# Attention sums and values of two head groups together on 64 by 32 TensorE tiles, in a kernel of attention and a two-layer MLP

## The chip, the cores and the metric

The kernel runs on one core of a Trainium2 chip. The metric is the device time of one execution in microseconds (us). Five runs of the kernel before gave 445.26 to 445.73 us, with a median of 445.7. Profiles come from one execution; in a profile "span" is the time from the first to the last instruction.

A core has five engines that run side by side, each working through its own list of instructions in order: TensorE (PE; its weight loads are shown as PEld), VectorE (DVE), ScalarE (ACT), GpSimd (POOL) and SyncE (SP). TensorE writes to PSUM, which here is cut into eight banks of 128 partitions by 512 fp32.

## What is computed

```
q_n = q / sqrt(mean(q*q) + 1e-6) * g_q        # the same for k; head_dim 64
attn = softmax(q_n k_n^T / 8)                 # 8 batches, 12 heads, 448 x 448
x    = (attn v) as [8*448 tokens, 768]
h    = x @ w_in                               # 768 x 2048
g    = max(h, 0) + alpha * min(h, 0)
out  = g @ w_out                              # 2048 x 768, fp32
```

All inputs are fp32. The kernel multiplies in fp16.

## The kernel before

**Groups.** Four heads make a group: two in each of two halves `g` of the head list (heads i and i+6 lie in different halves), and in each half two heads, `par` 0 and 1. There are G = 3 groups per batch and NG = 24 in all, counted y = 3*b + i. A key block j has 64 keys; J = 7 blocks make 448.

**One group's steps.** `load_qk` (L93, issued by SP) brings q and k. `square` (L128, POOL), `reduce` (L138, DVE), `root` (L146, ScalarE) and `scale` (L155, POOL) normalise them. They are then transposed, so that the head dimension lies on partitions: for y < TD = 8 on TensorE with 14 transposes and two evacuations (`turn`, L175), for later groups by two DMA transposes that SP issues (`turn_dma`, L165); `turn` is then only a multiply by the gain, in place, on DVE.

`score(y, j)` (L212) does four matmuls of 64 by 64, one for each head: keys go to PSUM partitions, the 448 queries are columns. The four use the four 64 by 64 tiles of the array at the same time. `soft` (L226) is one exp on ScalarE over 128 x 896, from PSUM to the fp16 tile `expT`. Score tiles have two PSUM buffers of two banks.

`den` (L250) sums over the keys, with weights of ones (64 columns, so each sum stands in 64 partitions); `attv` (L263) is the same with v as weights. Both are done by `over_keys` (L234): 28 matmuls of 64 by 64 by 448 columns, accumulated over j. Their result lies in `acc`, a two-bank buffer of which there is one. `log` and `invert` (L254, L259; ScalarE) make 1/sum as exp(-ln). DVE multiplies values by that into `xT`, the fp16 input of the MLP.

**MLP.** `up(b, ft)` (L307): six matmuls of 128 x 128 x 448 into one bank, ScalarE makes alpha*h, DVE takes the maximum and writes `gT`. `down(b0, t, oh)` (L322): 16 matmuls of 128 x 128 x 384 for 128 tokens and half `oh` of the output columns; DVE copies to `osb`, SP stores. Banks come from a pool of two (`psf`, tag "mm"), or, where `spare` is set, from `acc`.

**The order.** It is written out by a planner (L360 to L469), not found by a scheduler. The attention is cut into bursts. A burst has two score tiles (three where it also does sums or values from group 3 on), and possibly one group's sums (`dens`) or values (`avs`). Between bursts stand the `ups` and `downs` that the planner deals out by estimated costs (`gaps`, L434 to L462). There are 66 bursts. The burst in which batch 0's last group is summed is the "lead" (burst 11): there the MLP starts. Preparation of a later group is put into bursts by number: `prep` runs ahead of a burst, `post` behind it, `roots` and `jobs` inside. Lines 518 to 604 then emit all of it.

**Weights.** POOL issues the loads that convert fp32 to fp16: v of a batch (`load_v`, two requests), w_in in four parts by columns (`load_w_in`), w_out in four parts by rows (`load_w_out`). All of them go through one queue, whose transfers follow one another.

At the start TensorE multiplies idle data (`spin`, L348) between the first bursts.

Of the kernel before, what the change touches and what calls it, by code (L numbers as in the profile page):

```python
# [21 lines left out]
def kernel(  # L22
# [26 lines left out]
    TD = min(8, NG)  # L49
# [22 lines left out]
    ones = cst.tile([128, 64], FP16, name="ones", tag="ones")  # L72
# [3 lines left out]
    idle = cst.tile([128, S], FP16, name="idle", tag="idle")  # L76
    nc.vector.memset(idle, 0.0)
# [9 lines left out]
    gT = cst.tile([128, NF, W], FP16, name="gT", tag="gT")  # L87

# [26 lines left out]
    def load_w_in(c):  # L115
        nc.gpsimd.dma_start(
            out=w_in_sb[:, :, ts(c, FB)],
            in_=moe_w_in[:, ts(c, FB)].rearrange("(k p) f -> p k f", p=128),
        )

    def load_w_out(c):
        nc.gpsimd.dma_start(
            out=w_out_sb[:, ts(c, NF // 4), :],
            in_=moe_w_out[ts(c, DF // 4), :].rearrange("(t p) m -> p t m", p=128),
        )
# [86 lines left out]
    def score(y, j):  # L212
        qT, kT = qkT[y, "q"], qkT[y, "k"]
        sc = pss.tile([128, 2, 512], FP32, name="sc", tag="sc")
        for par in range(2):
            for g in range(2):
                nc.tensor.matmul(  # L217
                    out=sc[ds(64 * g, 64), par, :S].rearrange("p (j c) -> p j c", j=J),
                    lhsT=kT[ds(64 * par, 64), j, g, :],
                    rhs=qT[ds(64 * par, 64), :, g, :],  # L220
                    start=True,
                    stop=True,
                )
        scs[y, j] = sc

    def soft(y, j):  # L226
        if j == 0:
            expT[y] = att.tile([128, J, 2, S], FP16, name="expT", tag="expT")
        nc.scalar.activation(  # L229
            out=expT[y][:, j], in_=scs[y, j][:, :, :S], func=AF.Exp,  # L230
            scale=QK_SCALE, bias=expb[:, 0:1],
        )

    def over_keys(name, y, weights, spare=False):  # L234
        pool, tag = (pss, "sc") if spare else (psa, "acc")
        acc = pool.tile([128, 2, 512], FP32, name=name, tag=tag)
        e = expT[y]
        for j in range(J):
            for g in range(2):
                for par in range(2):  # L240
                    nc.tensor.matmul(  # L241
                        out=acc[ds(64 * par, 64), g, :S],
                        lhsT=weights(g, par, j),
                        rhs=e[ds(64 * g, 64), j, par, :],
                        start=(j == 0),
                        stop=(j == J - 1),
                    )
        return acc

    def den(y):  # L250
        dn = over_keys("dn", y, lambda g, par, j: ones[ds(64 * g, 64), :])
        rden[y] = dn

    def log(y):  # L254
        r = att.tile([128, 2, S], FP32, name="rden", tag="rden")
        nc.scalar.activation(out=r, in_=rden[y][:, :, :S], func=AF.Ln)  # L256
        rden[y] = r

    def invert(y):  # L259
        r = rden[y]  # L260
        nc.scalar.activation(out=r, in_=r, func=AF.Exp, scale=-1.0)  # L261

    def attv(y, spare=False, jobs=()):  # L263
        b, i = divmod(y, G)
        vv = vt[b]
        av = over_keys(
            "av", y, lambda g, par, j: vv[ds(64 * g, 64), 2 * i + par, j, :], spare
        )
        for f in jobs:
            f(y)  # L270
        if i == 0:
            xT[b] = att.tile([128, 2, G, S], FP16, name="xT", tag="xT")
        nc.vector.tensor_mul(  # L273
            out=xT[b][:, :, i, :], in0=av[:, :, :S], in1=rden[y]
        )
# [44 lines left out]
    osb = {}  # L320

    def down(b0, t, oh, jobs=(), spare=False):  # L322

        op = bank("op", spare)
        for ft in range(NF):
            nc.tensor.matmul(  # L326
                out=op[:, :OH],
                lhsT=gT[:, ft, ts(t, 128)],
                rhs=w_out_sb[:, ft, ds(oh * OH, OH)],
                start=(ft == 0),  # L330
                stop=(ft == NF - 1),
            )
        for f, a in jobs:
            f(*a)
        if oh == 0:
            osb[b0, t] = ffn.tile([128, DM], FP32, name="osb", tag="osb", bufs=3)
        o = osb[b0, t]
        nc.vector.tensor_copy(out=o[:, ds(oh * OH, OH)], in_=op[:, :OH])  # L338
        last = (b0, t) == (B - 2, J - 1)
        if oh == 1 or last:  # L340
            cols_out = ds(oh * OH, OH) if last else slice(None)
            for half in range(2):
                bb, j = divmod(2 * t + half, J)
                (nc.scalar if last and half else nc.sync).dma_start(
                    out=out4[b0 + bb, j, :, cols_out], in_=o[ds(64 * half, 64), cols_out]
                )
# [13 lines left out]
    bursts, dens, avs, first_in, last_in = [], {}, {}, {}, {}  # L360
    m = 0
    while m < NG * J or len(avs) < NG:
        n = len(bursts)
        if len(dens) > len(avs):
            avs[n] = len(avs)
        elif len(dens) < NG and last_in.get(len(dens), n) < n:
            dens[n] = len(dens)
            if dens[n] == G - 1:
                avs[n] = G - 1
        three = n in dens and dens[n] >= G or n in avs and avs[n] >= G  # L370
        count = min(3 if three else 2, NG * J - m)
        bursts.append([divmod(m + c, J) for c in range(count)])
        for y, j in bursts[n]:
            first_in.setdefault(y, n)
            if j == J - 1:
                last_in[y] = n
        m += count
    NB = len(bursts)
    den_at = {y: n for n, y in dens.items()}
    av_at = {y: n for n, y in avs.items()}  # L380
# [5 lines left out]
    def after(n, f, *a):  # L386
# [3 lines left out]
        y: max(n for n in range(first_in[y]) if n not in dens) for y in range(1, NG)  # L390
    }
    turn_at[2] = av_at[0]
    turns = {n: y for y, n in turn_at.items()}
    jobs = {}
    for y in range(G, NG):

        early = y < G + 2
        n = turn_at[y - 1] + (y == G) if early else max(d for d in dens if d <= turn_at[y] - 2)
        at(n - (8 if early else 5), load_qk, y)
        for nm in "qk":  # L400
            (after if early else at)(n - 2, square, y, nm)
            if early:
                after(n, reduce, y, nm)
            else:
                jobs.setdefault(n, []).append((reduce, (y, nm)))
        roots[n + 1 + (y == G + 1)] = y
# [7 lines left out]
    for b in range(B):  # L414
# [6 lines left out]
        tail = len(new) if b == B - 1 else 3 if b == 0 else 2 if odd else 1  # L421
# [3 lines left out]
    def cost(n):  # L425
        return (
            0.31 + 0.19 * len(bursts[n])
            + (1.35 if n in dens or n in avs else 0.0) + (0.9 if turns.get(n, TD) < TD else 0.0)
        )
# [6 lines left out]
    for b in range(B - 1):  # L436
# [3 lines left out]
        per = (mlp + sum(cost(n) for n in range(lo, hi))) / (hi - lo)  # L440
        clock = 0.0
        for n in range(lo, hi):
            clock += cost(n)
            free = True
            while ups or old or new:
# [14 lines left out]
                short = n in turns and len(gaps[n]) < 2  # L460
                if n < hi - 1 and not short and clock + ahead > per * (n - lo + 1):
                    break  # L462
# [42 lines left out]
    for nm in "qk":  # L505
        after(0, scale, 1, nm)
    after(0, load_w_in, 0)
    after(0, square, 2, "k")
    for nm in "qk":
        after(2, reduce, 2, nm)  # L510
    after(2, load_w_in, 1)
    after(5, load_w_in, 2)
    after(6, load_w_in, 3)
    for c in range(4):
        at(first - 2 + c, load_w_out, c)
    roots[4] = 2

    for n in range(NB):
# [5 lines left out]
        if lead:  # L524
            den(dens[n])
            attv(avs[n], True, (log, invert))
        for t in tiles[:2]:
# [4 lines left out]
            elif n == den_at[G - 1] - 1 and t == tiles[0]:  # L532
                begin(0)
# [4 lines left out]
        for t in tiles[:1] if wait else tiles[:2]:  # L538
# [3 lines left out]
        if n in avs and not lead:  # L542
            attv(avs[n])
        for t in tiles[2:]:
            score(*t)
            soft(*t)
        late = []
# [18 lines left out]
        for k, (f, a) in enumerate(gaps[n][:-1]):  # L566
            free = 2.3 if n in dens else 1.2 if n in avs else 0.1
            if clock >= free and not turns.get(n, TD) < TD and (
                not spare_at or k - spare_at[-1] > 2
            ):  # L570
                spare_at.append(k)
            clock += DOWN if f is down else UP
        ups_first = gaps[n] and gaps[n][0][0] is up
        if ups_first:
            for f, a in jobs.pop(n, ()):
                f(*a)
        turned = n in turns and turns[n] >= TD and ups_first
        if turned:
            turn(turns[n])
        for k, (f, a) in enumerate(gaps[n]):  # L580
# [3 lines left out]
            else:  # L584
                f(*a, spare)
                done += 1
                if late and done == late[0][0]:
# [3 lines left out]
            if n in turns and not turned and k == (  # L591
                0 if turns[n] >= TD or plain else max(min(1, len(gaps[n]) - 2), 0)
            ):
                turn(turns[n])
        if not gaps[n] and n in turns:
            turn(turns[n])
        for _, g, c in late:
# [37 lines left out]
```

The softmax here doesn't subtract the row's maximum and nothing guards it: scores larger than these inputs give would overflow.

## Time and profile before

| | |
|---|---|
| profiled execution, its own time | 445.36 us |
| its span | 443.6 us |
| median of five runs | 445.7 us |
| scores L217: matmuls, mean of one exp behind them | 672, 1007 ns |
| sums L241 (`dn`), values L241 (`av`): matmuls | 672, 672 |
| log, inverse: count, mean | 24 each, 928 and 953 ns |
| `turn` on TensorE: transposes | 112 |
| DVE: values times 1/sum, mean | 1091 ns |
| w_out: issue to landing, median | 20.7 us |

The page gives for each engine its busy time, then 40 equal slices of the span with the busy share of each in tenths. The longest chain of work that ends last has PE with 85% of the span, ScalarE with 8% and DVE with 4%; its largest lines are down (L326, 34%), up (L290, 29%), scores (8%), values (6%) and sums (6%). Matmuls are pipelined, and the profile models their ends: a matmul shown as 349 ns long can have a successor 47 ns later. So the time between starts is what counts on PE. Two groups of idle time look large and are not on that chain: POOL's 169.9 us ahead of `scale`, and DVE's 97.4 us waiting for a down.

### The profile page before, as it was taken

The page shows a single profiled execution, that of the slowest core. Times are in us where ns is not written, and L with a number is a line of the kernel's source. Part 1 is how long each engine was busy: PE and PEld are TensorE (multiplying, and loading weights), DVE is VectorE, ACT ScalarE, POOL GpSimd, SP SyncE. Part 2 cuts the span into 40 slices and gives each one's busy share as a digit, 9 for nine tenths or more (in the row PEclk, how much of TensorE's full clock was granted, in tenths as well). Part 3 has the DMA queues.
Part 4 walks back from the last instruction along what each step waited for, and adds up shares of the span by engine and source line. Part 5 has one row for each costly group of instructions (what it writes and reads, how often), then busy time and mean ns, then how long its engine had stood idle before and what let it go on. Part 6 is the DMA issues. An engine that isn't in the chain of part 4 may idle for free.

```text
span 443.6 us, 9091 instructions
## 1 busy us (share of the span) xinstructions
PE 424.9 (96%) x3837; PEld 228.9 (52%) x3837; DVE 206.8 (47%) x297; ACT 290.2 (65%) x401; POOL 170.8 (39%) x125
## 2 busy tenths in 40 slices
PE   7889998899999999999999999999999999999996
PEld 3344444555445555545555555545555545555563
DVE  3656654445554454454453554445553353234421
ACT  4998888667967676766875776767875767222300
POOL 4779946551554352362554351461533000000000
PEclk9899999999999999999999999999999999999999
DMA  8999999442973591771982583651732401111122
GB/s 196 230 237 245 233 252 199 120 91 72 190 159 69 129 178 46 161 124 38 196 183 62 141 163 62 161 126 36 140 78 51 63 2 38 37 35 37 35 72 71
DMA packets 60009, 52.77 MB, mean 119 GB/s; under 512 B 32688, under 2 KB 56512, under 8 KB 59968
## 3 DMA queue, kind: packets, MB, share of 16 engines
q1 hardware_dynamic: 47424, 39.27, 38.2%
q0 software_dynamic: 11808, 11.81, 16.7%
q10 hardware_dynamic: 736, 1.11, 1.0%
q8 instruction: 30, 0.49, 0.5%
q14 instruction: 11, 0.09, 0.1%
HBM read 45.62 MB, written 11.01 MB: 128 GB/s over the span
## 4 chain that ended last, share of the span: by engine, by line
PE 85%; ACT 8%; DVE 4%; DMA 1%; issue 0%; ACTq 0%
PE op L326 32%; PE hT L290 19%; PE hTa L290 10%; PE sc L217 8%; PE av L241 6%; PE dn L241 6%; ACT expT L229 4%; PE opa L326 2%; ACT ah L317 2%; DMA nat<-in_k_dram 1%; PE tps L193 1%; DVE gT L318 1%; PE spin L353 1%; ACT rden L256 1%; DVE kT L204 1%; DVE qT L202 1%
## 5 line engine op out<-in xcount | busy, mean ns | idle before, releaser
L229 ACT ACTIVATE expT<-sc,expb 128x896 f16<-128x896 f32 x168 | 158.5, 1007 | 18.4 <-PE sc L217 17.9
L326 PE MATMUL op<-w_out_sb,gT 128*128 128x384 f16 x848 | 145.6, 326 | 0.0
L158 POOL TENSOR_TENSOR qs<-nat,rr 128x896 f16<-128x896 f32 x44 | 78.1, 1795 | 169.9 <-issue 129.9
L326 PEld LDWEIGHTS <-gT 128*128 128x128 f16 x896 | 84.6, 98 | 63.5 <-issue 10.1
L290 PE MATMUL hT<-xT,w_in_sb 128*128 128x448 f16 x528 | 112.1, 353 | 2.4 <-DVE gT L318 2.4
L290 PEld LDWEIGHTS <-w_in_sb 128*128 128x128 f16 x768 | 73.4, 98 | 73.1 <-issue 9.1
L317 ACT ACTIVATE ah<-hT,cols 128x448 f16<-128x448 f32 x88 | 55.7, 634 | 62.9 <-PE hT L290 62.9
L318 DVE TENSOR_TENSOR gT<-hT,ah 128x448 f16<-128x448 f32 x88 | 54.8, 624 | 58.4 <-ACT ah L317 58.3
L338 DVE COPY osb<-op 128x384 f32<-128x384 f32 x53 | 29.5, 557 | 97.4 <-PE op L326 97.4
L135 POOL TENSOR_TENSOR sq<-nat 128x896 f32<-128x896 f32 x44 | 73.0, 1677 | 2.0 <-DMA nat<-in_k_dram 1.2
L217 PE MATMUL sc<-qT,kT 64*64 64x448 f16 x672 | 53.7, 362 | 7.0 <-DVE kT L204 3.3
L141 DVE TENSOR_REDUCE ss<-sq 128x14 f32<-128x896 f32 x48 | 49.9, 1076 | 6.9 <-ACT sq L133 6.3
L290 PE MATMUL hTa<-xT,w_in_sb 128*128 128x448 f16 x228 | 49.3, 352 | 0.0
L317 ACT ACTIVATE ah<-hTa,cols 128x448 f16<-128x448 f32 x38 | 24.1, 633 | 37.6 <-PE hTa L290 37.6
L318 DVE TENSOR_TENSOR gT<-hTa,ah 128x448 f16<-128x448 f32 x38 | 23.7, 624 | 33.8 <-ACT ah L317 33.8
L241 PE MATMUL av<-expT,vt 64*64 64x448 f16 x672 | 35.9, 349 | 1.8 <-ACT rden L256 1.8
L217 PEld LDWEIGHTS <-kT 64*64 64x64 f16 x672 | 18.6, 105 | 36.8 <-issue 25.1
L273 DVE TENSOR_TENSOR xT<-av,rden 128x896 f16<-128x896 f32 x24 | 26.2, 1091 | 21.6 <-PE av L241 19.8
L241 PE MATMUL dn<-expT,ones 64*64 64x448 f16 x672 | 36.0, 349 | 0.2 <-DVE gT L318 0.2
L241 PEld LDWEIGHTS <-vt 64*64 64x64 f16 x672 | 20.6, 107 | 13.3 <-issue 2.6
L241 PEld LDWEIGHTS <-ones 64*64 64x64 f16 x672 | 20.9, 107 | 11.1 <-issue 0.6
L261 ACT ACTIVATE rden<-rden 128x896 f32<-128x896 f32 x24 | 22.9, 953 | 0.7
(40 smaller groups left out, 136.1 us busy)
## 6 DMA issues: line engine op xcount, KB each, us to landing
out_dram<-osb SPq DMA_DIRECT2D x54, 192.0 KB, 2.7
nat<-in_q_dram SPq DMA_DIRECT2D x46, 224.0 KB, 4.7
nat<-in_k_dram SPq DMA_DIRECT2D x46, 224.0 KB, 5.4
vt<-in_v_dram POOLq DMA_DIRECT2D x16, 336.0 KB, 7.7
w_in_sb<-in_moe_w_in_dram POOLq DMA_DIRECT2D x4, 768.0 KB, 13.9
w_out_sb<-in_moe_w_out_dram POOLq DMA_DIRECT2D x4, 768.0 KB, 20.7
nat<-in_q_dram ACTq DMA_DIRECT2D x2, 224.0 KB, 4.8
nat<-in_k_dram ACTq DMA_DIRECT2D x2, 224.0 KB, 6.2
```

Source lines behind the costliest of these rows:

```text
L135: nc.gpsimd.tensor_mul(out=sqf, in0=src, in1=src)
L141: nc.vector.tensor_reduce(out=ss_t[y][:, "qk".index(nm)].rearrange("p h j -> p (h j)").unsqueeze(2), in_=sqs[y, nm], axis=AXIS_X, op=ALU.add,)
L158: eng.tensor_mul(out=t.rearrange("p j h d -> p h j d"), in0=nat[y, nm], in1=rr_t[y][:, "qk".index(nm)].unsqueeze(3).broadcast_to((128, 2, ...
L217: nc.tensor.matmul(out=sc[ds(64 * g, 64), par, :S].rearrange("p (j c) -> p j c", j=J), lhsT=kT[ds(64 * par, 64), j, g, :], rhs=qT[ds(64 * ...
L229: nc.scalar.activation(out=expT[y][:, j], in_=scs[y, j][:, :, :S], func=AF.Exp, scale=QK_SCALE, bias=expb[:, 0:1],)
L241: nc.tensor.matmul(out=acc[ds(64 * par, 64), g, :S], lhsT=weights(g, par, j), rhs=e[ds(64 * g, 64), j, par, :], start=(j == 0), stop=(j == ...
L273: nc.vector.tensor_mul(out=xT[b][:, :, i, :], in0=av[:, :, :S], in1=rden[y])
L290: nc.tensor.matmul(out=hT[:, :S], lhsT=w_in_sb[:, g * G + i, ts(ft, 128)], rhs=xT[b][:, g, i, :], start=(i == 0 and g == 0), stop=(i == G ...
L317: nc.scalar.activation(out=ah, in_=hT[:, :S], func=AF.Copy, scale=alpha_sb[:, ft : ft + 1])
L318: nc.vector.tensor_max(out=gT[:, ft, ds((b & 1) * S, S)], in0=hT[:, :S], in1=ah)
L326: nc.tensor.matmul(out=op[:, :OH], lhsT=gT[:, ft, ts(t, 128)], rhs=w_out_sb[:, ft, ds(oh * OH, OH)], start=(ft == 0), stop=(ft == NF - 1),)
L338: nc.vector.tensor_copy(out=o[:, ds(oh * OH, OH)], in_=op[:, :OH])
```

## The change

1. `over_keys` takes one or two groups. With two, the eight heads are spread over eight tiles of 64 rows by 32 columns (four column strips, two halves g), so each head has 32 partitions of the result. `den` of a pair is then one set of seven key blocks with eight matmuls each. Values of a pair take two sets: even columns of v (`half` 0) into `acc`, odd columns (`half` 1) into the two "mm" banks. A single group (the third of a batch) uses the eight tiles with the two halves of each head's 64 columns. Groups of a batch are done as a pair and a single one.
2. `score` does eight matmuls of 64 by 32 instead of four of 64 by 64.
3. In a burst with a pair's values, the third score stands between the two halves. `expT` has three buffers instead of two, `osb` two instead of three.
4. The rows of w_in are loaded in another order, since the columns of x stand in another order in `xT`: three requests per part. w_out is loaded by column halves.
5. TD is 6 instead of 8: groups 6 and 7 (the first two of the third batch) are also transposed by DMA. The bursts at which groups are loaded, squared, rooted and turned are set anew. There are 73 bursts; the lead is burst 10. The first down stays in burst 17, values of the pair (3, 4) stand in burst 18.
6. The planner's costs, and the choice of downs and ups that use the spare bank, follow the new bursts; `idle` is now a part of `gT`.

```
-    TD = min(8, NG)
+    TD = min(6, NG)
+    EB = 3
...
     def load_w_in(c):
+        src = moe_w_in[:, ts(c, FB)].rearrange("(g r) f -> g r f", g=2)
+        dst = w_in_sb[:, :, ts(c, FB)].rearrange("p (g i) f -> p g i f", g=2)
+        for g in range(2):
+            nc.gpsimd.dma_start(
+                out=dst[:, g, 0:2], in_=src[g, :256].rearrange("(p e) f -> p e f", e=2)
+            )
         nc.gpsimd.dma_start(
-            out=w_in_sb[:, :, ts(c, FB)],
-            in_=moe_w_in[:, ts(c, FB)].rearrange("(k p) f -> p k f", p=128),
+            out=dst[:, :, 2], in_=src[:, 256:].rearrange("g p f -> p g f")
         )
     def load_w_out(c):
+        oh, half = divmod(c, 2)
         nc.gpsimd.dma_start(
-            out=w_out_sb[:, ts(c, NF // 4), :],
-            in_=moe_w_out[ts(c, DF // 4), :].rearrange("(t p) m -> p t m", p=128),
+            out=w_out_sb[:, ts(half, NF // 2), ds(oh * OH, OH)],
+            in_=moe_w_out[ts(half, DF // 2), ds(oh * OH, OH)].rearrange(
+                "(t p) m -> p t m", p=128
+            ),
         )
...
+        for c in range(2):
+            for par in range(2):
+                for g in range(2):
+                    nc.tensor.matmul(
+                        out=sc[ds(64 * g + 32 * c, 32), par, :S].rearrange(
+                            "p (j c) -> p j c", j=J
+                        ),
+                        lhsT=kT[ds(64 * par, 64), j, g, ts(c, 32)],
...
+    def over_keys(accs, ys, weights):
+        if len(ys) == 2:
+            heads = [(y, par, 0) for y in ys for par in range(2)]
+        else:
+            heads = [(ys[0], par, c) for par in range(2) for c in range(2)]
         for j in range(J):
-            for g in range(2):
-                for par in range(2):
+            for h, (y, par, c) in enumerate(heads):
+                for g in range(2):
                     nc.tensor.matmul(
-                        out=acc[ds(64 * par, 64), g, :S],
-                        lhsT=weights(g, par, j),
-                        rhs=e[ds(64 * g, 64), j, par, :],
+                        out=accs[g][ds(32 * h, 32), :S],
+                        lhsT=weights(g, y, par, c, j),
+                        rhs=expT[y][ds(64 * g, 64), j, par, :],
...
+    def attv(ys, half, spare=False, jobs=()):
+        b, i = divmod(ys[0], G)
+        v2 = vt[b].rearrange("p h j (d e) -> p h j d e", e=2)
+        def weights(g, y, par, c, j):
+            h = 2 * (y - G * b) + par
+            if len(ys) == 1:
+                return vt[b][ds(64 * g, 64), h, j, ts(c, 32)]
+            return v2[ds(64 * g, 64), h, j, :, half]
+        if half:
+            av, accs = None, [psf.tile([128, 512], FP32, name="avb", tag="mm") for _ in range(2)]
...
+        x, r = xT[b][:, :, i + half, :], rden[ys]
+        if half:
+            for g in range(2):
+                nc.vector.tensor_mul(out=x[:, g], in0=accs[g][:, :S], in1=r[:, g])
+        else:
+            nc.vector.tensor_mul(out=x, in0=av[:, :, :S], in1=r)
...
     after(0, load_w_in, 0)
-    after(2, load_w_in, 1)
-    after(5, load_w_in, 2)
-    after(6, load_w_in, 3)
+    after(5, load_w_in, 1)
+    after(7, load_w_in, 2)
+    after(8, load_w_in, 3)
     for c in range(4):
-        at(first - 2 + c, load_w_out, c)
+        after(first + c // 2, load_w_out, c)
...
         if n in avs and not lead:
-            attv(avs[n])
-        for t in tiles[2:]:
+            attv(avs[n], 0)
+        for t in tiles[len(first_tiles) :]:
             score(*t)
             soft(*t)
+        if n in avs and len(avs[n]) == 2:
+            attv(avs[n], 1)
```

## Prediction

> **What bounds the kernel now.** I read the busy shares first, then the slices, then the idle time of the engines by releaser, then TensorE's order of time around one ordinary burst, and last the first 80 us by themselves.
>
> ```profile
> PE 424.9 (96%) x3837; PEld 228.9 (52%) x3837; DVE 206.8 (47%) x297; ACT 290.2 (65%) x401; POOL 170.8 (39%) x125
> PE   7889998899999999999999999999999999999996
> ...
> PEclk9899999999999999999999999999999999999999
> DMA  8999999442973591771982583651732401111122
> ```
>
> TensorE is busy and at full clock from the ninth slice on; DMA is full only in the first seven slices. So there are two stages with different limits. A busy PE need not be an efficient one, so I look at starts, in the timeline of PE:
>
> ```profile
> 201.92 1.30 PE L290 MATMUL hTa<-xT,w_in_sb 128*128 128x448 f16 x6
> 203.05 1.30 PE L290 MATMUL hT<-xT,w_in_sb 128*128 128x448 f16 x6
> 204.28 0.57 PE L217 MATMUL sc<-qT,kT 64*64 64x448 f16 x8
> 204.68 1.49 PE L241 MATMUL av<-expT,vt 64*64 64x448 f16 x28
> 206.01 0.36 PE L217 MATMUL sc<-qT,kT 64*64 64x448 f16 x4
> 206.30 2.77 PE L326 MATMUL op<-w_out_sb,gT 128*128 128x384 f16 x16
> ```
>
> From start to start: six full-array matmuls take 1.13 (189 ns each); 28 matmuls of 64 by 64 take 1.33, which is seven rounds of four tiles at once, 189 ns a round. That is one round per 448 columns, with nothing between. Only where the array changes its tiling is there more: 1.23 instead of 1.13 ahead of the scores (+0.10), 0.29 instead of 0.19 behind them (+0.10). Hence 0.2 us per burst. Here only fewer rounds help. The windows give the same:
>
> ```profile
> 21.00:41.00 20.00, 16.71 (x266) 9.45 (x264) 11.86 (x13) 19.04 (x25) 17.54 (x12) 1.00 1.16 234
> 38.10:41.10 3.00, 3.00 (x64) 1.75 (x64) 1.90 (x2) 2.28 (x4) 3.00 (x3) 1.00 1.16 269
> 46.00:83.00 37.00, 32.85 (x346) 17.57 (x349) 20.20 (x30) 29.10 (x43) 24.50 (x18) 1.00 0.99 201
> 83.00:400.00 317.00, 314.47 (x2880) 170.24 (x2873) 147.89 (x214) 217.37 (x298) 110.85 (x72) 1.00 0.49 103
> ```
>
> (columns: busy PE, PEld, DVE, ACT, POOL, then clock, DMA share, GB/s.) From 83 to 400 TensorE idles 2.5 of 317 us; from 21 to 41 ScalarE is the full one (19.0 of 20), and from 46 to 83 nobody is quite full but DMA (0.99).
>
> **The change, part by part.** All sums are against the profiled execution: span 443.6, its own time 445.36, so 1.8 lie outside the span; the median of the runs is 445.7.
>
> *Denominators of two groups together.* Before, 24 sets of seven rounds (1.32 us in the chain of waits); after, a set for the pair and one for the single group, 16 sets. If a round of eight 64 by 32 tiles takes the 189 ns of a round of four, eight sets go: 10.6 us. One of these (batch 0) lies where ScalarE sets the pace; there what counts is that one logarithm and one inverse fall away, 0.93 + 0.95 = 1.9. So 7 x 1.32 + 1.9 = 11.2. Values stay at three sets per batch, scores at one round each: twice the matmuls for the same columns. ScalarE also saves 7 x 1.9 later, worth nothing, since PE is the bound there.
>
> *The price of a round of eight.* No row shows eight tiles. Near rows: 47 ns per matmul with its weights, and within a round the single records of the trace start 3.4 ns apart; by these a round of eight stays at 189. [...]
>
> *Turns of groups 6 and 7 by DMA.* TensorE loses two sets of 14 transposes, 0.78 each (91.72 to 92.50): -1.6, and with the first a stall of 1.3 at 80.8 (score behind kT). Added: four DMA transposes, 2.9 to 3.3 us each to land, issued by SP behind the loads of group 8 and ahead of those of group 9 and of the outputs; and two in-place DVE multiplies of 0.57, against the four evacuations of 0.62 to 0.68 that go. Cover: roots move to bursts 15 and 17, use is in 19 and 22. If cover fails, the score of group 6 waits, at most the length of two transposes, 6 us.
>
> *More, smaller bursts.* The plan gives 73 instead of 66; those in between MLP work are 8 more: 8 x 0.2 = +1.6.
>
> *Third score between the two value halves, odd half in the two MLP banks.* The score needs the first exp done: 1.0 against 1.3 of even values, hidden. The first down behind uses the spare bank, whose even values DVE clears (1.09) while the odd half runs (1.32): hidden, by 0.2. Queued behind a late clear would be that down only. The odd clear (two of 0.62) ends before the next up. `osb` with two buffers instead of three: a tile is rewritten two tiles later, over 10 us, and an output lands in 2.7; `expT` with three only frees. Together zero, with 0.2 x 7 = 1.5 as the other end; below zero it can't be, as it removes no PE work.
>
> *Weights.* Twelve requests instead of four for w_in, which POOL issues after bursts 0, 5, 7, 8 (before 0, 2, 5, 6), and w_out by column halves, rows of 1536 B in HBM; the first down needs two of its four parts instead of all. POOL's queue now runs: w_in, two w_out parts, scaling of group 5, two w_out parts, squares of group 6, then the values of batch 1. Before, these values stood ahead of w_out:
>
> ```profile
> 41.03 1.36 POOL L110 DMA_DIRECT2D vt<-in_v_dram  x2
> 42.38 2.28 POOL L122 DMA_DIRECT2D w_out_sb<-in_moe_w_out_dram  x3
> 51.45 0.80 POOL L122 DMA_DIRECT2D w_out_sb<-in_moe_w_out_dram  x1
> ```
>
> The single records of that queue show it without a gap from 13 to 71.4, where w_out ended; the first down began at 72.8. So DMA sets when batch 1 can be attended to. After: same bytes, all of them needed for the pair (3, 4) at burst 18. Transfer end: 71.4, plus smaller packets (w_out 134 ns per 1536 B, w_in 98 per 1024, so about 80 per 768: 4096 x 80 - 2048 x 134 over 16 engines = 3.3), plus 1.7 since the first w_in goes behind a square, plus about 1 of gaps from the later issues: 77.5, an estimate; 72 if POOL is early, 84 if the gaps of later w_in issues and two early transposes all add.
>
> *When does PE want it?* The lead burst started at 38.3 behind the exp of group 2; less 1.9 is 36.4. To the values of (3, 4) PE then has: 2.6 sums and values of group 2, 17.4 up (92 x 0.189), 19 scores and a set of sums 4.9, turns 1.6, one down 2.6, some 11 changes of tiling 2.2: 31.3. So 67.7 without stalls, 72 with those that stage has now (4.8 from 46 to 83, from the records). The values land at 77.5: PE waits 5 to 10 us in burst 18. Behind that wait stand the third score, the odd half and the second down, and ScalarE and DVE run dry with them. This eats most of what the start wins.
>
> *The sum.* From the values of (3, 4) on I compare with before's 82.8 (sums of group 5 begin, 360.8 to the end). Extra: one down 2.6, both value sets 2.6, four scores 0.8, changes 1.6. Less: six sets of sums 7.9, one turn 0.8. 360.8 + 7.6 - 8.7 = 359.7. Span 77.5 + 359.7 = 437.2, time **439.0**.
>
> **Rivals.**
> 1. *No DMA wait*: transfers end by 67.7 to 72, PE sets the start as well: 427.4 to 431.7, with 1.8 outside 429 to 433.5. For it: rows of q and k could be less pressing. Against: a queue without gaps and a DMA share over 1 from 21 to 41.
> 2. *PE is not supplied fast enough* (slower). The place is the four bursts with sums or values of each batch: 440 matmuls in 20.1 us, 22 per us. [...] In favour of it: nothing in the trace excludes it. Against: PE never idles with "issue" as its reason, at lead not even after 56 matmuls in a row.
> [...]
> 4. *The change does nothing*, because a round of eight runs as two of four: 448 rounds become 896; excluded as "no change", it would be 439 + 406 x 0.19 = 516. Little chance: the four tiles of a round already run at once.
>
> **Chances.** Forecast (435 to 443): 0.45. Rival 1: 0.20. Rival 3: 0.18, of which 0.07 faster, 0.05 same, 0.06 slower. Rivals 2 and 4: 0.17. Faster by over 0.2% (what a measurement of this kernel can tell from no change): 0.72; same 0.05; slower 0.23. The range takes the first three, 428 to 452; the far slow cases are left out.
>
> **What would show it.** [...] PE idle at burst 18, released by the DMA of vt, ending near 77.5; no such wait means rival 1. After it PE as full as now, with 16 sets of sums and 84 transposes. PE idle with "issue" as releaser in the sums would make the prediction wrong; so would scores waiting for kT of group 6.

## The result and the profile after

The changed kernel took **442.45 us** (median of 24 runs, 439.12 to 446.4) against 445.52 (44 runs, 444.92 to 446.4): ratio 0.993, 95% interval 0.9916 to 0.9943. It is faster by 3.1 us, where 6.7 were forecast. The profiled execution lies above the median: 445.62 us, with a span of 443.8. Here and below the ratios leave out single executions in a slower state at a lower granted clock (3 of the 25 of the change, 1 of the 6 of the last kernel); the medians do not.

The page after, in the rows shown of before:

```profile
PE 416.5 (94%) x5381; PEld 215.5 (49%) x5381; DVE 210.9 (48%) x303; ACT 277.4 (62%) x385; POOL 176.1 (40%) x133
PE   7778888699999899999999999999999999999996
...
PEclk9999999699999999999999999999999999999999
DMA  8999999968617881388219861577028301111122
```

TensorE has 8.4 us less work and the same span. Its slices 2 to 6 and 8 are emptier than before, and the eighth slice has a granted clock of 6 tenths, which no slice of before had. The windows of before, repeated after:

```profile
21.00:41.00 20.00, 14.73 (x377) 7.59 (x376) 11.63 (x14) 14.89 (x20) 19.71 (x16) 1.00 1.12 218
38.10:41.10 3.00, 1.92 (x71) 0.97 (x77) 2.50 (x3) 0.14 (x1) 2.98 (x3) 1.00 1.13 217
46.00:83.00 37.00, 28.08 (x347) 13.34 (x352) 16.54 (x26) 27.60 (x42) 23.93 (x18) 0.96 1.18 190
83.00:400.00 317.00, 313.87 (x4222) 162.60 (x4207) 156.23 (x223) 209.47 (x288) 116.27 (x77) 0.99 0.51 109
```

Behind 83 us PE is as full as it was. From 21 to 41 ScalarE fell from 19.0 to 14.9 of 20 and now waits, like PE, for others, while GpSimd rose from 17.5 to 19.7; from 46 to 83 PE fell from 32.9 to 28.1 of 37. The gain is in the late stage, the loss in the start.

A burst with a pair's values in the timeline of PE, in the late stage:

```profile
127.66 0.57 PE L229 MATMUL sc<-qT,kT 64*32 64x448 f16 x16
128.05 1.51 PE L257 MATMUL av<-expT,vt 64*32 64x448 f16 x56
129.38 0.37 PE L229 MATMUL sc<-qT,kT 64*32 64x448 f16 x8
129.56 1.51 PE L257 MATMUL avb<-expT,vt 64*32 64x448 f16 x56
131.00 2.29 PE L359 MATMUL opa<-w_out_sb,gT 128*128 128x384 f16 x13
```

From start to start, 56 matmuls take 1.33, so a round of eight tiles takes 190 ns, as a round of four did; the score between the halves takes 0.18 and waits for nobody. Only the change to the full array costs more (1.44 from `avb` to `opa`). The first such burst, at the pair (3, 4):

```profile
76.64 0.57 PE L229 MATMUL sc<-qT,kT 64*32 64x448 f16 x16
79.56 0.42 PE L257 MATMUL av<-expT,vt 64*32 64x448 f16 x1 [2.35 <-DMA vt<-in_v_dram]
81.62 2.81 PE L257 MATMUL av<-expT,vt 64*32 64x448 f16 x55 [1.65 <-DMA vt<-in_v_dram]
83.86 0.95 PE L229 MATMUL sc<-qT,kT 64*32 64x448 f16 x8
84.23 2.83 PE L257 MATMUL avb<-expT,vt 64*32 64x448 f16 x56
86.99 1.31 PE L359 MATMUL opa<-w_out_sb,gT 128*128 128x384 f16 x7
```

PE comes at 77.2 and waits for v until 81.6; one matmul, for which the first half of v is enough, starts at 79.6. Then the same work takes 5.4 us instead of 2.9: the rounds take about 370 ns, twice the usual, until 86.5. The window from 79.8 to 86.5 has a granted clock of 0.50. When the clock fell, at 79.7, PE had idled for 2.35 us, from 77.2 to 79.6, and the second wait, of 1.65, lies inside the 6.8 us for which it stays at 0.50. In before the clock is at 0.50 once while PE has work, for 3.4 us from 13.8, behind gaps of 0.94, 0.38 and 0.78. In the 3.4 us ahead of each fall PE was busy for 1.7 in before and for 1.1 here.

From the end of the odd half (86.99) to the end are 356.8 us; the prediction had 359.7 - 2.84 = 356.9. **So the steady sum was right, and the whole error of the profiled execution, 6.6 us, lies before 87 us.**

In part that is luck. The sum took over the idle time that before has in its late stage, 2.5 us, most of it first layers of the MLP waiting for `gT`. In the change most of that is gone, and one wait of about the same size, which the prediction had at nothing, stands in its place. It is seen in DVE and PE:

```profile
142.63 1.88 DVE L190 TENSOR_SCALAR kT<-kT,gain 128x896 f16<-128x896 f16 x1 [6.27 <-DMA kT<-qs]
146.02 1.29 PE L323 MATMUL hTa<-xT,w_in_sb 128*128 128x448 f16 x6 [2.46 <-DVE xT L308]
```

DVE stands for 6.3 us at a group's keys, whose DMA transpose takes 7.6 us from issue to landing, and the product with 1/sum for which PE waits is queued behind it.

### The profile page after: what moved, and what is told of

It reads as the page before. It is cut to its first block, busy times and chain, and to the rows that moved or that the text cites. A ratio compares the mean times of both kernels' runs of the same rounds, so it can differ in the third digit from the quotient of the medians.

```text
span 443.8 us, 12178 instructions
## 1 busy us (share of the span) xinstructions
PE 416.5 (94%) x5381; PEld 215.5 (49%) x5381; DVE 210.9 (48%) x303; ACT 277.4 (62%) x385; POOL 176.1 (40%) x133
## 4 chain that ended last, share of the span: by engine, by line
PE 75%; DMA 9%; ACT 5%; issue 5%; DVE 2%; POOL 2%; SPq 1%; POOLq 0%; DVEq 0%; ACTq 0%
PE op L359 25%; PE hT L323 17%; PE hTa L323 9%; PE sc L229 7%; PE opa L359 5%; DMA vt<-in_v_dram 5%; PE av L257 4%; PE dn L257 4%; ACT expT L243 4%; PE avb L257 2%; DMA kT<-qs 2%; DMA nat<-in_k_dram 1%; DMA nat<-in_q_dram 1%; POOL qs L169 1%; PE tps L204 1%
## 5 line engine op out<-in xcount | busy, mean ns | idle before, releaser
L359 PE MATMUL op<-w_out_sb,gT 128*128 128x384 f16 x736 | 127.1, 326 | 0.5 <-issue 0.5
L359 PEld LDWEIGHTS <-gT 128*128 128x128 f16 x896 | 84.6, 98 | 67.4 <-issue 13.7
L351 DVE TENSOR_TENSOR gT<-hT,ah 128x448 f16<-128x448 f32 x86 | 53.6, 624 | 63.5 <-ACT ah L350 63.5
L229 PE MATMUL sc<-qT,kT 64*32 64x448 f16 x1344 | 54.4, 355 | 9.5 <-ACT expT L243 6.6
L371 DVE COPY osb<-op 128x384 f32<-128x384 f32 x46 | 25.6, 556 | 71.0 <-PE op L359 71.0
L229 PEld LDWEIGHTS <-kT 64*32 64x32 f16 x1344 | 16.0, 89 | 39.9 <-issue 34.8
L257 PE MATMUL av<-expT,vt 64*32 64x448 f16 x896 | 26.0, 363 | 4.9 <-DMA vt<-in_v_dram 4.0
L257 PEld LDWEIGHTS <-vt 64*32 64x32 f16 x1344 | 20.5, 97 | 19.1 <-DMA vt<-in_v_dram 4.8
L308 DVE TENSOR_TENSOR xT<-av,rden 128x896 f16<-128x896 f32 x16 | 17.4, 1090 | 23.3 <-PE av L257 20.8
L359 PE MATMUL opa<-w_out_sb,gT 128*128 128x384 f16 x160 | 27.7, 326 | 0.0
L257 PE MATMUL dn<-expT,ones 64*32 64x448 f16 x896 | 24.5, 349 | 1.2 <-DVE kT L215 0.6
L190 DVE TENSOR_SCALAR kT<-kT,gain 128x896 f16<-128x896 f16 x18 | 15.7, 873 | 12.3 <-DMA kT<-qs 12.3
```

What stands on the lines that cost most here:

```text
L229: nc.tensor.matmul(out=sc[ds(64 * g + 32 * c, 32), par, :S].rearrange("p (j c) -> p j c", j=J), lhsT=kT[ds(64 * par, 64), j, g, ts(c, 32)] ...
L257: nc.tensor.matmul(out=accs[g][ds(32 * h, 32), :S], lhsT=weights(g, y, par, c, j), rhs=expT[y][ds(64 * g, 64), j, par, :], start=(j == 0), ...
L308: nc.vector.tensor_mul(out=x, in0=av[:, :, :S], in1=r)
L351: nc.vector.tensor_max(out=gT[:, ft, ds((b & 1) * S, S)], in0=hT[:, :S], in1=ah)
L359: nc.tensor.matmul(out=op[:, :OH], lhsT=gT[:, ft, ts(t, 128)], rhs=w_out_sb[:, ft, ds(oh * OH, OH)], start=(ft == 0), stop=(ft == NF - 1),)
```

## The experiments

The first theory (A): the forecast's gain is there, and the start gives it back by the wait for v, with the low clock behind it. The rivals: the wait is only the last of several late things, among them the start's ScalarE and GpSimd (B); and PE is not supplied with instructions fast enough (C), since the profile shows PE idle with "issue" as its reason, which before did not. Intervals of ratios are at 95%, all against the kernel before.

**Take the wait away: no load of batch 1's v.** Batch 1 uses the v of batch 0, so this kernel leaves out one load and its values of batch 1 are other numbers.

```
     def load_v(b):
+        if b == 1:
+            vt[1] = vt[0]
+            return
```

> The changed kernel without the load of batch 1's v: batch 1 uses the v of batch 0 (its output is therefore another one). In the changed kernel's profile TensorE idles 4.5 us at burst 18 for that load, and the 16 rounds behind it run at half clock, 2.6 us more. Theory A (this wait and the clock that it costs are what the prediction sized wrongly): 442.5 less 5 to 7, that is 435.5 to 437.5, no half clock. Rival B (the transfers as a whole bind; another one takes the place of the wait): 440.5 to 442.5, with TensorE idle ahead of a down.

Measured 441.14 us (4 runs, 438.76 to 442.72), ratio 0.9917 (0.9894 to 0.994). That is 1.3 less than the change itself, with overlapping intervals, and within the range that B expects. But the sign that B named, PE idle ahead of a down, is missing in the start of its profile; what stands there are stops of 1.6 and 0.7 us with "issue" as the reason. What replaces the wait, or was beside it, matters.

**Take the wait away and keep the work: ask for v ahead of w_out.**

```
-    for b in range(1, B):
+    after(9, load_v, 1)
+    for b in range(2, B):
         at(av_at[G * b] - 6, load_v, b)
```

> The changed kernel with the load of batch 1's v put ahead of the four w_out parts in GpSimd's queue (it was behind them); all bytes are still moved. Theory A: the values land near 56, w_out's second part near 70 (first down at 73.9 today), its fourth near 81 (second down near 80): at most 1 to 2 us of wait are left and the clock stays, 436 to 438.5. Rival B: the wait moves in full to the second or first down, 441 to 443.

Measured **440.4 us** (6 runs, 439.79 to 443.96), ratio 0.9904 (0.9879 to 0.9929). This lies between what A and B expected. The last packet of v ended at 54.7 and that of w_out at 77.8; no PE wait names either. In its place stand waits without a releaser; the timeline at two of them:

```profile
33.14 0.36 PE L229 MATMUL sc<-qT,kT 64*32 64x448 f16 x3 [0.36 <-ACT expT L243]
36.01 0.37 PE L229 MATMUL sc<-qT,kT 64*32 64x448 f16 x5 [2.50 <-issue]
...
81.00 0.76 PE L257 MATMUL avb<-expT,vt 64*32 64x448 f16 x24
82.33 0.95 PE L257 MATMUL avb<-expT,vt 64*32 64x448 f16 x32 [0.56 <-issue]
```

PE stops amid a group of like matmuls whose inputs the matmuls ahead have read already. That speaks for C. Behind the first halt the granted clock is 0.50 from 36.9 to 40.1, so that a halt costs more than its own length.

**Keep the clock up while PE waits.** 18 products of idle data ahead of the values in burst 18.

> The changed kernel with 18 extra matmuls on idle data (3.4 us at full clock) ahead of the values of groups 3 and 4 in burst 18, where TensorE waits. They compute nothing that is used. Theory A: they lie inside the wait and keep the clock; the values then run at 189 ns a round instead of 374: 1.5 to 2.6 us faster, 440 to 441. If the half clock has another cause, or the wait is mostly shorter than 3.4 us: 442.5 to 444.

Measured 442.37 us (4 runs, 441.01 to 443.68), ratio 0.9932 (0.9913 to 0.9951).

```profile
76.03 3.58 PE L386 MATMUL spin<-gT,ident 128*128 128x448 f16 x18
80.52 0.36 PE L257 MATMUL av<-expT,vt 64*32 64x448 f16 x1 [0.91 <-DMA vt<-in_v_dram]
83.05 1.51 PE L257 MATMUL av<-expT,vt 64*32 64x448 f16 x55 [2.17 <-DMA vt<-in_v_dram]
84.22 0.54 PE L229 MATMUL sc<-qT,kT 64*32 64x448 f16 x8
```

With PE kept busy, the rounds behind the wait run at full clock (1.00 from 79 to 90; 55 matmuls in 1.17 instead of 2.24): that the idle time causes the slow rounds is shown. But v came later still (83.05), and the median is that of the change. The low clock alone doesn't explain the median.

**Four times the sums, in both kernels.** The same seven rounds are run four times in each set; each time overwrites the one before, so that the result stays. After has 56 matmuls in seven rounds, before 28. (The edit of after; before's does the same.)

```
-        over_keys(
-            (dn[:, 0], dn[:, 1]), ys, lambda g, y, par, c, j: ones[ds(64 * g, 64), :]
-        )
+        for _ in range(4):
+            over_keys(
+                (dn[:, 0], dn[:, 1]), ys, lambda g, y, par, c, j: ones[ds(64 * g, 64), :]
+            )
```

> The changed kernel with each of the 16 sets of sums done four times over (the last overwrites the others, so the result is the same): 28 rounds of eight tiles in a row, 448 matmul and weight-load instructions. If TensorE is supplied as fast as it computes: 5.3 us a set at 189 ns a round, 16 x 3.97 = 63.5 more, 505 to 508. Rival C (instructions come in too slowly): idle time without any wait inside a set, 6 us and more per set, over 515.

> The kernel before with each of its 24 sets of sums done four times over (64 by 64 tiles, four matmuls a round): 28 rounds in a row as in the fourfold sums of the changed kernel, but 224 instructions instead of 448. Rival C, as page of 256 instructions (the halts without a wait in the other runs fall on each 256th instruction, whatever it is): a page lasts 6 us here, not 3, so at most a few halts: 24 x 3.97 = 95.3 more, 541 to 545, where the changed kernel had 20 us beyond its 63.5. If instead long sets as such are slow (score buffers, clock, ScalarE): 20 us or more beyond, over 560.

After: 526.52 us (one run), about 84 more than the change's median; 48 added sets of 1.32 us account for 63.5. Before: 539.25 us (one run), 94 more; 72 added sets account for 95.3. So the long sets of 64 by 64 tiles cost what their rounds cost, and those of 64 by 32 cost 20 us beyond. The profile of the latter has 20.8 us of halts and the granted clock at 0.50 in three stretches of 13.7 us in all; the wait for v is gone in it, so these don't simply add. PE's waits in the two, first after, then before:

```profile
PE dn L257 <- issue: 11.1, 6, 3.3
PE sc L229 <- ACT expT L243: 6.5, 11, 1.5
PE op L360 <- issue: 6.5, 1, 6.5
```

```profile
PE sc L217 <- ACT expT L229: 3.9, 7, 1.3
PE sc L217 <- DVE kT L204: 3.3, 4, 1.3
PE hT L290 <- DVE gT L318: 2.3, 5, 0.7
```

(columns: us in total, times, the longest.) The columns streamed are alike; twice the instructions for them make the halts. I count PE's records, matmuls and weight loads, from the first on and call them rows. In after with four times the sums, the halts without a wait stand at rows 701, 1213, 1469, 1725, 2491, 2747, 5559, 7349, 7605, 9393, 11439: within 14 rows all of these lie a multiple of 256 apart (a few records may be missing). The page's row of the instruction queue gives the same unit; here before, then after:

```profile
q8 instruction: 30, 0.49, 0.5%
```

```profile
q8 instruction: 42, 0.69, 0.7%
```

42 packets of 16 KB for 10,762 rows are 256 rows each, and 30 for before's 7,674 are too: I call the 256 rows of a packet a page. In the change packets ended at 32.9, 38.8 and 241.1, and PE went on after its three halts 1.5, 1.5 and 1.3 us behind these ends, at 34.4, 40.3 and 242.4. C is right in kind: the supply comes by pages, and a halt comes where a page has been run through before the next is there.

**The tiles alone: before, with scores, sums and values on 64 by 32 tiles**, each group by itself as before.

> The kernel before, with each 64 by 64 matmul of scores, sums and values split into two of 64 by 32: same rounds, twice the instructions, nothing else changed. Theory A (a round of eight costs what a round of four does): 445 to 446. Rival C (supply): 447 to 452, with idle time in the sums or scores that no wait explains. If a round of eight took 200 ns: 504 x 11 ns = 5.5 more, 451.

Measured 449.42 us (4 runs, 448.83 to 449.74), ratio 1.0096 (1.0079 to 1.0113). Same rounds, twice the attention's instructions: +3.9 us, in the range of C. By the starts of PE the offset is there at 49 us (the first down at 76.28 instead of 72.78) and stays 3.5 to the end. It is made of three pieces: a stop of 1.44 amid 14 like transposes, which the profile puts down to another engine but which stands at row 957, 256 after 701; the clock at 0.50 behind it, from 38.2 to 41.5 (some 1.7); and a halt of 0.38 at row 1213. So instructions are dear in the start and free behind it, and a round at 200 ns, which would have added all along, is excluded.

**Scores on 64 by 64 tiles in the changed kernel, without and with the early v.** In `score`, `n = 64` takes the place of 32 and of the loop over `c`.

> The changed kernel with scores as before, four matmuls of 64 by 64; sums and values stay on 64 by 32. 1344 fewer instructions for TensorE, but the array changes its tiling inside a burst too: some 60 changes of 0 to 0.1 us. Rival C: the halts in the first 45 us shrink, 2 to 3 us gained, against 0 to 6 us of changes: 440 to 445. If halts count for nothing: 442.5 to 448.5.

> Both edits: batch 1's v ahead of w_out, and scores on 64 by 64. The first alone gave 440.4. If halts and the wait are separate costs, the gains add: 437.5 to 440. If the change of tiling costs 0.1 us each: 443 or more.

Measured 446.84 us (7 runs, 443.42 to 448.73), ratio 1.0023 (0.9993 to 1.0053), and 443.87 (7 runs, 441.45 to 444.57), ratio 0.996 (0.9943 to 0.9977). The first lies in the range for halts that count for nothing, the second where changes of tiling cost 0.1 each. Yet the start is better: no halt around 33 us, sums of group 2 at 36.9 (after: 38.7), odd half of (3, 4) done at 82.6 and, with early v, 78.2. The rest is worse by 7.4 us (364.2 from the end of the odd half to the end with the late v, 356.8 in the change). Some 1.7 of this is the clock, at 0.50 from 143.4 to 146.8 behind a wait of 2.35 for `xT`; without idle time and halved clock 6.3 are left, and 6.6 between the two kernels with early v. The timeline of PE, scores on 64 by 64:

```profile
124.03 0.57 PE L228 MATMUL sc<-qT,kT 64*64 64x448 f16 x8
124.53 1.52 PE L254 MATMUL av<-expT,vt 64*32 64x448 f16 x56
125.98 0.38 PE L228 MATMUL sc<-qT,kT 64*64 64x448 f16 x4
126.30 1.52 PE L254 MATMUL avb<-expT,vt 64*32 64x448 f16 x56
```

Against the burst above, from start to start: 0.50 for 0.39, 1.45 for 1.33, 0.32 for 0.18. Each change between 64 by 64 and 64 by 32 costs 0.11 to 0.14, like one to the full array; two or three of them in four bursts of each of seven batches make 63, or 6.3 to 7.6 us at 0.10 to 0.12 each. That is why scores had to take the new tiling too.

**Turns of groups 6 and 7 back on TensorE.**

```
-    TD = min(6, NG)
+    TD = min(8, NG)
...
-        turned = n in turns and gaps[n] and (turns[n] >= TD or turns[n] < 2 * G)
+        turned = n in turns and gaps[n]
```

> The changed kernel with groups 6 and 7 transposed on TensorE again (TD is 8), everything else as changed. Prediction's step: two sets of transposes, 1.6 us, and up to 1.3 of wait come back: 444 to 445.5. Rival: without their transfers in the full stage the values of batch 1 land up to 4 us earlier, and GpSimd doesn't wait 11 us for them: 440 to 442.5.

Measured 444.84 us (10 runs, 442.39 to 447.91), ratio 0.9997 (0.997 to 1.0024): 2.4 slower than the change, which fits what was forecast for this part, 1.6 and a stall of 1.3. It is no more than a fit: v landed 0.9 earlier, as the rival said in kind, the profiled execution (443.17) is faster than that of the change, and the ten runs spread over 5.5 us.

**64 by 64 scores only where they change no tiling**: up to the lead, and later in bursts without sums or values; without and with early v.

```
+    narrow = {
+        t for n in range(den_at[G - 1] + 1, NB)
+        if n in dens or n in avs for t in bursts[n]
+    }
...
+        n = 32 if (y, j) in narrow else 64
```

> Scores on 64 by 64 tiles in the start (up to the lead burst) and, later, in every burst without sums or values; on 64 by 32 only beside sums or values, so that no burst changes its tiling more often than in the changed kernel. Supply theory: with 64 by 64 scores the start had no halt without a wait (the odd half of (3, 4) ended at 82.3 instead of 87.0), and behind it the time is the 356.8 us of the changed kernel, since the 7 us that 64 by 64 scores cost there were changes of tiling: 439 to 441.5. If the earlier start was chance or another wait takes its place: 442 to 443.5. If 64 by 64 scores cost the 7 us for another reason than the changes of tiling: 444.5 or more.

> The same scores, and the values of batch 1 are asked for ahead of w_out. Supply theory: odd half ends at 78.2 as with all scores on 64 by 64 and early values, then 355.4 us as with early values alone: 433.6 of span, 434.5 to 437 us. If the two halves of the start (supply and wait for values) are not separate losses, no more than the better one: 439.5 to 441. If the tiling of scores costs time in itself: 442.5 or more.

Measured 442.7 us (12 runs, 438.13 to 444.44), ratio 0.9921 (0.9893 to 0.9949), and **439.67** (5 runs, 438.09 to 441.04), ratio 0.9862 (0.9846 to 0.9877). I had expected 439 to 441.5 and 434.5 to 437: both missed. The tiling was understood (no loss of 7 us: behind the odd half, without idle time and halved clock, PE takes 353.8 and 354.1, in the change 353.7). The start was earlier, but this was given back. The first kernel still has the wait for v (3.1) and the late one for `xT` (2.5), with a halved clock behind each. The second loses it at one place. The timeline of the second kernel:

```profile
76.53 1.51 PE L258 MATMUL av<-expT,vt 64*32 64x448 f16 x56
77.98 0.38 PE L230 MATMUL sc<-qT,kT 64*32 64x448 f16 x8
78.17 1.14 PE L258 MATMUL avb<-expT,vt 64*32 64x448 f16 x36
81.86 1.31 PE L258 MATMUL avb<-expT,vt 64*32 64x448 f16 x20 [2.55 <-issue]
```

A halt of 2.6 us at row 1723, with slow rounds behind it (20 matmuls in 1.24, the clock at 0.50 from 81.5 to 84.9). The first of the two kernels, with the same instructions for PE, runs over row 1723 without a halt, 3.5 us after its wait for v: the wait had covered the halt.

**Move the pages: 132 more rows at the very start.** The kernel just told, with its first 22 idle products cut in four; `spin(22, 4)` streams the same columns.

> The kernel before this one, with the 22 idle products at the very start cut into four parts of 112 columns each: the same columns, 132 more PE rows ahead of everything else. Nothing that the later code does or waits for is changed, only where each 256th row falls: the boundaries behind rows 957 and 1723 (halts of 1.3 and 2.7 us without a wait in the profiled execution) now fall into the sums of group 2 and into the middle of the even values of (3, 4), where the page that ends there takes longer to run through. Supply theory: halts at 957 and 1723 are gone, other ones only at rows of the form 190 + 256 k; 436 to 438.5 us. If the halts belong to those instructions and not to their place in the stream, they stay with the instructions (then 132 rows later): 439 to 440.5. If halts only move to other boundaries: 438.5 to 440.5, and the profile shows them there.

Measured **438.31 us** (6 runs, 435.01 to 443.48), ratio 0.9809 (0.9773 to 0.9845), the best kernel of all. The timeline:

```profile
76.55 1.11 PE L258 MATMUL av<-expT,vt 64*32 64x448 f16 x34
80.83 1.31 PE L258 MATMUL av<-expT,vt 64*32 64x448 f16 x22 [3.17 <-issue]
81.57 0.95 PE L230 MATMUL sc<-qT,kT 64*32 64x448 f16 x8
```

My expectation was wrong in one half. The halts did not go: they are again at rows 957 (0.5 us) and 1723 (3.2 us), exactly those of the kernel before. But other instructions stand there now: a `dn` for an `hT`, and an `av`, 132 rows ahead of the `avb` that had stopped. So the halt belongs to the place in the stream, not to the instruction, nor to what the instruction waits for; that is shown. The median lies in the range that I had given for no halts, which is luck: the profiled execution (440.24) still has them. Nor does the clock explain it, since three runs at a granted clock of 1.0 took 438.1 to 439.7 without the shift, and two took 435.0 and 435.9 with it. The two intervals just meet.

The records of the instruction queue give the duration. In this kernel PE ran over row 1470 at 71.7; the page's packet ran from 78.1 to 79.2; PE went on at 80.8, at row 1723. Up to 85 us the packet begins 2.8 to 6.4 us behind such a row, later mostly within 1.4. The DMA engines are fully busy in the former time (share 1.24 from 46 to 83) and half in the latter (0.51 from 83 to 400 in the change). That the packet stands behind the data's packets is my guess from these two shares; it was not tested by taking data away.

## Why the prediction was right and wrong

*Right:* the price of a round of eight (190 ns, 23.6 per matmul); 16 sets of sums and 84 transposes; the hidden third score; turns by DMA, as far as the runs can tell; the work of the steady sum, with the luck told above; the wait for v in burst 18, and that it "eats most of what the start wins". The range, up to 452, allowed for rounds of 200 ns, which no run shows: they took 190. That excludes rival 4 too, whose 406 rounds are the 448 of the change less the 42 of the start that ScalarE bounds.

*Wrong:* the step that failed is **"Transfer end: 71.4, plus smaller packets ..., plus 1.7 ..., plus about 1 of gaps from the later issues: 77.5"**. v's last packet ended at 81.3, 3.8 later. The packets' term was right (w_out and v took from 51.2 to 81.3 = 30.1, against 26.5 before: +3.6 for 3.3 forecast). So was the 1.7: w_in ended at 49.5 instead of 47.6. The term "about 1 of gaps" was mis-sized. This stretch began at 51.2 instead of 44.9, 6.3 later; 1.8 of it is w_in, and 4.5 stand where the prediction had 1. GpSimd gives the reason, in the timeline of its queue:

```profile
46.23 3.33 POOL L169 TENSOR_TENSOR qs<-nat,rr 128x896 f16<-128x896 f32 x2 [2.65 <-ACT rr L164]
49.51 1.82 POOL L131 DMA_DIRECT2D w_out_sb<-in_moe_w_out_dram  x2
51.34 3.35 POOL L169 TENSOR_TENSOR qs<-nat,rr 128x896 f16<-128x896 f32 x2
54.62 1.81 POOL L131 DMA_DIRECT2D w_out_sb<-in_moe_w_out_dram  x2
56.44 3.33 POOL L146 TENSOR_TENSOR sq<-nat 128x896 f32<-128x896 f32 x2
59.71 1.37 POOL L112 DMA_DIRECT2D vt<-in_v_dram  x2
```

The first w_out request stands behind two scalings that wait for a root; the prediction's list of the queue has one pair of scalings, between the w_out parts. The twelve w_in requests had also taken GpSimd 8.8 us, where four took 3.5. So the queue ran dry for 1.7, from 49.5 to 51.2. Before asked for v at 41.0, and its first packets ran from 44.9, while w_in's went on to 47.6: the transfers of this queue can overlap, by 2.7 there, and the change lost that.

A term was put at nothing without a reason: the clock behind the wait, 2.5 us (5.4 for 2.9). 4.1 at the restart of PE (81.6 against 77.5) and 2.5 are the 6.6 by which the profiled execution misses.

For the median, 3.4 over the forecast, the split is not the same, and part of it stays open. Over the runs the clock lost (1 - granted clock, times span) averages 2.9 us in the change and about 1.1 in before: some 1.8 of the 3.4 goes with the clock. The two runs of the change at 0.998 took 439.12 and 440.56. Without the wait the gain is 1.3 to 2.0 more, not the 6.6 that the profiled execution lost: what is late next is the supply, which the forecast had among rivals of 0.17 together, in the wrong form, as a rate per matmul. Inside a page no limit shows at 23.6 ns per matmul over 56; the halts stand where a page was run through before the next was there, 2.3 us in the profile of the change and 20.8 in that of the kernel with four times the sums. The prediction's lead at 36.4 failed in part by the same; PE in the change:

```profile
34.40 0.37 PE L229 MATMUL sc<-qT,kT 64*32 64x448 f16 x5 [1.27 <-issue]
38.67 1.12 PE L257 MATMUL dn<-expT,ones 64*32 64x448 f16 x33 [0.55 <-DVE kT L215]
40.32 0.76 PE L257 MATMUL dn<-expT,ones 64*32 64x448 f16 x23 [0.53 <-issue]
```

It came at 38.7, 2.3 late: 1.27 of this is a halt and 0.55 a wait for keys. Behind the wait for v this cost nothing, and without the wait it does.

What was not settled: which share of a single run's time is clock and which is supply (the runs of most variants spread over 3 to 8 us, those of before over 1.5), what holds a page's packet back, and why the last kernel gains over the one before it.

## What to carry to other kernels

Smaller tiles that run at the same time make more instructions for the same columns: count rows of the instruction list per us, and ask at each dense stretch whether 256 of them (3.0 us in these 64 by 32 sets) last longer than the next packet takes at that time (in the last kernel it began 2.8 to 6.4 us behind the boundary up to 85 us, later mostly within 1.4). In the change the dense stretches halted for 1.8 us in the start, where DMA was full, and for 0.5 behind 87 us, where it was half busy. When a wait is to be removed, look what else is late at that very time (here a page), since the wait covers it; and reckon with the clock, which fell to 0.50 behind stops of 2.35, 2.50 and 2.55 us here. A transfer's end is not the sum of its packets: follow the issuing engine's queue through what stands ahead of each request, as here the gaps decided.

## What the runs showed of the hardware that was not expected

- TensorE halts at 256-row boundaries of its instructions where the code is dense, mostly while DMA is full: 0.2 to 6.5 us, independent of the instruction that stands there. In dense code of 64 by 32 tiles a page lasts 3.0 us (128 matmuls of 23.6 ns), in 64 by 64 6.0; only the former halted in the kernels with long sets.
- A halved clock for 3.4 or 6.8 us came with gaps of 2.35 us and more, once with two of 0.5 and 1.4, and from 13.8 in before with three of 0.94, 0.38 and 0.78; but not with the change's gap of 2.46 at 146. After the wait for v the rounds took 350 to 375 ns instead of 190, for some 13 rounds.
- A change between 64 by 64 and 64 by 32 tiles costs 0.11 to 0.14 us, as much as one between either and the full array.
